# Splitting float64 weights into two fp32 parts: four VectorE steps in SBUF and two on GpSimd for each of twelve blocks, without PSUM banks

## The chip, the core and the metric

The kernel runs on one core of one Trainium2 chip. The metric is the time of one execution in microseconds (us) on the device. The profile names the engines PE (TensorE matmul), PEld (TensorE weight load), DVE (VectorE), ACT (ScalarE), POOL (GpSimd) and SP (SyncE, which issues most DMAs); SPq and ACTq are DMA-issuing instructions on those queues. SBUF is the on-chip memory of 128 partitions, PSUM the eight banks into which TensorE writes.

## What is computed

Banded attention for 8 batches, 8 heads, 576 positions and head size 64, followed by a gated feed-forward block:

```python
# attention: B, H, S, D = 8, 8, 576, 64
scores = q @ k.T / sqrt(D)           # heads 0-3: last 32 positions; heads 4-7: every 4th of the last 128
attn = softmax(where(mask, scores, -1e9))
x = (attn @ v).transpose(0, 2, 1, 3).reshape(B, S, 512)
# gated block: d_ff = 1024
h = maximum(x @ w_in, 0)
u, v = h[..., :512], h[..., 512:]
v_n = (v - mean(v)) / sqrt(var(v) + 1e-6)
v_s = einsum('ts,bsd->btd', w_spatial, v_n) + b_spatial[None, :, None]
out = (u * v_s) @ w_out
```

q, k, v, w_spatial and b_spatial are float32. w_in (512x1024) and w_out (512x512) are float64: they come from a float32 array times a numpy float64 scalar.

## The kernel before

**Two-part products.** Every matmul of the gated block runs in three passes over operands that were split into a high part `hi`, rounded to the matmul's fp32r format, and a low part `lo`, what is left: high by high, high by low, low by high. Activations are split with one copy (ACT) and one subtraction (DVE or POOL). Where a name ends in `h` or `l` it is such a part: `wih`/`wil` of w_in, `woh`/`wol` of w_out, `wth`/`wtl` of w_spatial, `xth`/`xtl` of the attention's output, `vnh`/`vnl` of the normalised v, `gh`/`gl` of the gated product.

**The float64 weights.** `weight` (line 276) splits one block of 128 rows by 512 columns. There are twelve: w_in's second half (`half` 1, used by the v tiles), blocks 1 to 4 below; its first half (`half` 0, used by the gate), blocks 5 to 8; and w_out, blocks 9 to 12. A block's 512 KB come by DMA into one of four `stage` buffers (`weight_in`, line 265; w_in in two transfers of 256 KB). ACT scales the words' upper halves (L295); DVE shifts the exponent into place (L297) and puts the sign back (L299), which gives `g`, the number without its last bits; ACT rounds `g` to `hi` (L334); DVE cuts `g` down to its power of two (L305); the lower words, times that power and 2**-52, are what `g` lacks; `lo` is the difference `g - hi` plus that rest. Blocks 1 to 6 do the lot on DVE (L297, L299, L305, L322, then the difference through the helper at L256 and the sum L328), with one `mid` buffer in SBUF and two PSUM banks. Blocks 7 to 12 (`pool=True`) do the last three steps on POOL (L312, L259, L318) after another ACT copy (L310), with two `mid` buffers and one PSUM bank.

**The stages around it.** The first batch has a start-up: q, k and v of two head groups and the weights are loaded, scores and softmax run (`unit`, three for each head group; POOL multiplies by the reciprocal sum at L489, PE transposes at L494, L520 multiplies by the values), the result is split (`evacuated`: xth by ACT at L546, xtl by DVE through L256), the v tiles are multiplied (`v_tile`, L572 and L586), normalised (L604 to L611) and split (L618, and POOL through L259), the gate follows (`gate`, L645 for u, L656 to L658 for the spatial product, L661 and L667) and the projection (`project`, L681). Of batch 1 the units are interleaved with the gate of batch 0, and so on.

**What sets the order.** Every piece of work is a generator, a strand with a rank. `Timeline` runs them against a table of costs, takes the strand whose next step can start earliest (start plus 0.2 times rank) and emits its instructions; each engine then executes in the order of emission. Buffers are handed out by tags (`stage`, `mid`, `bank`, `kqv` and so on). The tag `wk` has no buffer: it bounds how many blocks that use it are in work at once. So a changed cost or tag in `weight` changes the order of all engines' queues, not only of its own instructions. The spatial product cannot start before the bias is in (`bias`, line 362): its DMA of `b_sp` needs a `stage` buffer, and so an earlier block that gave its buffer back.

Of the kernel before, what the change touches and what calls it, by code (L numbers as in the profile page):

```python
# [121 lines left out]
def tile_banded_attention_gated_moe(  # L122
# [52 lines left out]
    def bufs(tag, shape, n, pool=const):  # L175
# [12 lines left out]
            wk=[None] * 1,  # L188
# [43 lines left out]
    ident = const.tile([P, P], F32, name="ident")  # L232
    make_identity(nc, ident)
# [42 lines left out]
    def weight(key, hi, lo, dtype, pool=False):  # L276

        yield [("in", *key)]
        yield "mid" if dtype == F32 else "mid mid bank" if pool else "wk mid bank bank"
        mid = yield ACT, 0.66  # L280
        *slot, mid = (mid[:1], mid[1:]) if len(mid) == 4 else (mid,)
        big = staged[key]
        if dtype == F32:
            w = big[1][:, :512]
            nc.scalar.copy(hi, w)
            yield DVE, 0.68
            sub(lo, w, hi)
            tl.give(big, *mid)
            tl.done(*key)
            return  # L290
        words = big[1][:, :1024].rearrange("p (c w) -> p w c", w=2)
        t, g, f = (m[1].bitcast(U32) for m in mid)


        nc.scalar.activation(f.bitcast(F32), words[:, 1], AF.Copy, scale=2.0**-112)  # L295
        yield DVE, 0.6
        nc.vector.tensor_scalar(t, f, 3, 0x7FFFFFFF, op0=ALU.logical_shift_left, op1=ALU.bitwise_and)  # L297
        yield DVE, 0.68
        nc.vector.scalar_tensor_tensor(g, f, 0x80000000, t, op0=ALU.bitwise_and, op1=ALU.bitwise_or)  # L299
        tl.add(key[-1] * 0.01, rounded(hi, g.bitcast(F32), ("hi", *key)))  # L300

        low = words[:, 0].bitcast(U32)
        p = t if pool else f
        yield DVE, 0.43 if pool else 0.6
        nc.vector.tensor_scalar(p, g, 0xFF800000, None, op0=ALU.bitwise_and)  # L305
        t, g, f, p = (m.bitcast(F32) for m in (t, g, f, p))
        if pool:
            tl.give(mid[2])
            yield ACT, 0.66
            nc.scalar.activation(words[:, 0], low, AF.Copy, scale=2.0**-52)  # L310
            yield POOL, 1.3
            nc.gpsimd.tensor_mul(t, p, words[:, 0])  # L312
            tl.give(big)
            yield [("hi", *key)]
            yield POOL, 1.3
            gsub(g, g, hi)
            yield POOL, 1.3
            nc.gpsimd.tensor_add(lo, t, g)  # L318
            tl.give(*mid[:2])
        else:  # L320
            yield DVE, 0.68
            nc.vector.scalar_tensor_tensor(f, low, 2.0**-52, p, op0=ALU.mult, op1=ALU.mult)  # L322
            tl.give(big)
            yield [("hi", *key)]
            yield DVE, 0.68
            sub(t, g, hi)
            yield DVE, 0.68
            nc.vector.tensor_add(lo, f, t)  # L328
            tl.give(*mid, *slot[0])
        tl.done(*key)  # L330
# [377 lines left out]
    for half in (1, 0):  # L708
        cols = slice(half * NF, half * NF + NF)
        for c in range(NC):  # L710

            heads = [c // 2 * 4 + c % 2 + n for n in (0, 2)]
            src = tuple(w_in[h * D : h * D + D, half] for h in heads)
            halves[half, c] = weight_in(("wi", half, c), src)
            r = -1.05 if half else -0.5
            tl.add(r + c * 0.05, weight(("wi", half, c), wi[0][:, c, cols], wi[1][:, c, cols], w_in.dtype, half == 0 and c > 1))
# [6 lines left out]
    for c in range(NC):  # L723
        tl.add(0.3, weight(("wo", c), wo[0][:, c, :], wo[1][:, c, :], w_out.dtype, True))
# [87 lines left out]
```

## Time and profile before

| what | us |
|---|---|
| time before, median of 3 runs | 581.32 |
| lowest and highest of the runs | 580.89 and 618.86 |
| time of the profiled execution (its span) | 580.3 |
| PE busy | 550.5 (95% of the span) |
| DVE busy | 317.0 (55%) |
| ACT busy | 248.5 (43%) |
| POOL busy | 139.2 (24%) |

The page gives for the profiled execution no time but the span, from its first to its last instruction; the median of the runs is 1.0 us above it. A row of the timeline reads: start, duration, engine, line, operation, output <- inputs, shape and type, count, and in brackets how long the engine had been idle and what ended that.

### The profile page before, as it was taken

The page shows a single profiled execution, that of the slowest core. Times are in us where ns is not written, and L with a number is a line of the kernel's source. Part 1 is how long each engine was busy: PE and PEld are TensorE (multiplying, and loading weights), DVE is VectorE, ACT ScalarE, POOL GpSimd, SP SyncE. Part 2 cuts the span into 40 slices and gives each one's busy share as a digit, 9 for nine tenths or more (in the row PEclk, how much of TensorE's full clock was granted, in tenths as well). Part 3 has the DMA queues.
Part 4 walks back from the last instruction along what each step waited for, and adds up shares of the span by engine and source line. Part 5 has one row for each costly group of instructions (what it writes and reads, how often), then busy time and mean ns, then how long its engine had stood idle before and what let it go on. Part 6 is the DMA issues. An engine that isn't in the chain of part 4 may idle for free.

```text
span 580.3 us, 18315 instructions
## 1 busy us (share of the span) xinstructions
PE 550.5 (95%) x7971; PEld 509.1 (88%) x7971; DVE 317.0 (55%) x765; ACT 248.5 (43%) x630; POOL 139.2 (24%) x163
## 2 busy tenths in 40 slices
PE   9788358999999999999999999999999999999997
PEld 7576358999999989998999989999999989999997
DVE  2789977244863376434863376444863476444411
ACT  2855686433444344434444344433444433423321
POOL 2110988001520032201420032201430132201000
PEclk9969577999999999999999999999999999999999
DMA  9986585431366104631355104641364012101011
GB/s 230 198 213 172 156 216 109 126 84 42 85 143 148 45 4 118 174 84 42 85 150 143 42 6 120 171 82 42 85 177 117 31 36 61 43 1 42 1 42 41
DMA packets 97444, 56.66 MB, mean 98 GB/s; under 512 B 78290, under 2 KB 87506, under 8 KB 97364
## 3 DMA queue, kind: packets, MB, share of 16 engines
q1 hardware_dynamic: 88148, 46.06, 32.7%
q10 hardware_dynamic: 9216, 9.44, 4.6%
q8 instruction: 62, 1.02, 0.7%
q14 instruction: 18, 0.15, 0.1%
HBM read 46.04 MB, written 9.44 MB: 96 GB/s over the span
## 4 chain that ended last, share of the span: by engine, by line
PE 82%; DVE 6%; DMA 5%; SPq 3%; POOL 1%; issue 1%; ACT 1%; ACTq 0%; DVEq 0%; POOLq 0%
PE bank L656 18%; PE bank L645 17%; PE bank L681 16%; PE bank L572 14%; PE bank L520 6%; PE bank L438 4%; PE bank L494 3%; DMA kqv<-in_vw_dram 2%; SPq L414 2%; PE bank L586 2%; PE bank L658 1%; PE bank L657 1%; DMA stage<-in_w_in_dram 1%; DMA kqv<-in_qT_dram 1%; DMA out_dram<-ob 1%
## 5 line engine op out<-in xcount | busy, mean ns | idle before, releaser
L608 POOL TENSOR_TENSOR rs<-rs,halfneg 128x1 f32<-128x1 f32 (+1 forms) x40 | 30.9, 776 | 244.5 <-DVE rs L606 244.5
L645 PE MATMUL bank<-xth,wih 128*128 128x288 f32 x256 | 80.1, 313 | 1.8 <-ACT p L464 1.8
L656 PE MATMUL bank<-wth,vnh 128*128 128x288 f32 x256 | 79.0, 309 | 0.0
L661 DVE TENSOR_TENSOR ur<-ur,bank 128x288 f32<-128x288 f32 x64 | 29.0, 453 | 87.9 <-PE bank L658 87.8
L645 PE MATMUL bank<-xtl,wih 128*128 128x288 f32 x256 | 76.7, 300 | 0.1
L645 PE MATMUL bank<-xth,wil 128*128 128x288 f32 x256 | 76.5, 299 | 0.0
L681 PE MATMUL bank<-gh,woh 128*128 128x288 f32 x256 | 76.3, 298 | 0.0
L656 PE MATMUL bank<-wtl,vnh 128*128 128x288 f32 x256 | 76.2, 297 | 0.0
L656 PE MATMUL bank<-wth,vnl 128*128 128x288 f32 x256 | 76.2, 297 | 0.0
L681 PE MATMUL bank<-gl,woh 128*128 128x288 f32 x256 | 75.7, 296 | 0.1
L681 PE MATMUL bank<-gh,wol 128*128 128x288 f32 x256 | 75.6, 295 | 0.0
L489 POOL TENSOR_TENSOR p<-p,rv 128x384 f32<-128x384 f32 x48 | 41.0, 855 | 78.4 <-DVE rv L487 71.5
L667 ACT CAST gh<-ur 128x288 fp32r<-128x288 f32 x64 | 27.6, 432 | 65.7 <-DVE ur L661 65.7
L645 PEld LDWEIGHTS bank<-xth,wih 128*128 128x128 f32 x256 | 49.1, 192 | 3.8 <-ACT p L464 2.2
L572 PE MATMUL bank<-wih,xth 128*128 128x512 f32 x128 | 51.2, 400 | 0.3 <-DVE xtl L256 0.3
L572 PE MATMUL bank<-wil,xth 128*128 128x512 f32 x128 | 50.6, 396 | 0.0
L572 PE MATMUL bank<-wih,xtl 128*128 128x512 f32 x128 | 50.4, 394 | 0.0
L645 PEld LDWEIGHTS bank<-xtl,wih 128*128 128x128 f32 x256 | 49.3, 192 | 0.4 <-issue 0.3
L656 PEld LDWEIGHTS bank<-wth,vnh 128*128 128x128 f32 x256 | 48.7, 190 | 0.6
L645 PEld LDWEIGHTS bank<-xth,wil 128*128 128x128 f32 x256 | 49.2, 192 | 0.0
L681 PEld LDWEIGHTS bank<-gl,woh 128*128 128x128 f32 x256 | 48.5, 189 | 0.6 <-DVE gl L256 0.3
L656 PEld LDWEIGHTS bank<-wtl,vnh 128*128 128x128 f32 x256 | 48.8, 191 | 0.2
(105 smaller groups left out, 1167.6 us busy)
## 6 DMA issues: line engine op xcount, KB each, us to landing
kqv<-in_vw_dram SPq DMA_DIRECT2D x128, 144.0 KB, 4.2
out_dram<-ob ACTq DMA_DIRECT2D x64, 144.0 KB, 1.8
kqv<-in_kT_dram SPq DMA_DIRECT2D x30, 304.0 KB, 3.4
kqv<-in_qT_dram SPq DMA_DIRECT2D x30, 288.0 KB, 4.2
stage<-in_w_in_dram SPq DMA_DIRECT2D x16, 256.0 KB, 5.6
stage<-in_w_out_dram SPq DMA_DIRECT2D x4, 512.0 KB, 3.4
stage<-in_w_spT_dram SPq DMA_DIRECT2D x5, 288.0 KB, 3.2
kqv<-in_kT_dram SPq DMA_DIRECT2D x2, 192.0 KB, 3.6
```

The costliest lines, as they stand in the source:

```text
L414: nc.sync.dma_start(dst[j * D : j * D + D, :, n, :], src[n * QB : n * QB + KW, :, j, :])
L438: nc.tensor.matmul(s[j][q * QB : q * QB + QB, e, :], kq[r, WIN + S :].rearrange("p (u n i t) -> p u t n i", n=2, i=QB, t=US)[:, u, g // 2 ...
L489: nc.gpsimd.tensor_mul(flat, flat, rv.unsqueeze(2).broadcast_to([P, 2 * US, KW]))
L494: nc.tensor.transpose(pp[:, e, :], p[:, e].rearrange("p j k -> p (j k)"), ident)
L520: nc.tensor.matmul(acc[j][1][1][i * D : i * D + D, (g - h * HB) * QB : (g - h * HB + 1) * QB], v[r, g, :], probs[b, G, u][1][r, e, q * QB ...
L572: nc.tensor.matmul(pm, x[a][:, c, cols], wi[w][:, c, NF:], start=c == 0 and n == 0, stop=c == NC - 1 and n == 2)
L608: nc.gpsimd.tensor_tensor(rs[:m], rs[:m], halfneg[:m], op=ALU.pow)
L645: nc.tensor.matmul(pu, wi[w][:, c, fs], x[a][:, c, ts], start=n == 0, stop=n == 3 * NC - 1)
L656: nc.tensor.matmul(pv, vn[c][a][:, fs], wt[w][:, c, ts], start=n == 0, stop=False)
L661: nc.vector.tensor_mul(ur, ur, pv)
L667: nc.scalar.copy(gated[0][:, f, ts], ur)
L681: nc.tensor.matmul(po, wo[w][:, f, ds], gated[a][:, f, ts], start=n == 0, stop=n == 3 * NC - 1)
```

## The change

- All twelve blocks take one path. ACT scales the upper words into a `mid` buffer in SBUF (not into a PSUM bank); DVE does four steps (shift, sign, power of two, lower words times the power), each with all inputs and its output in SBUF; POOL does the difference and the last sum.
- Each block needs two `mid` buffers and a `wk` tag and no bank. There are two `wk` tags, not one, and all twelve blocks use them; the ACT copy L310 and the POOL multiplication L312 are gone. The table's costs change with it.
- A third path (`sums=True`, with matmuls against `plus` and `minus`) is in the code, but both calls pass `False`, so that it emits nothing.
- The identity is drafted in the first `ob` buffer; `plus` and `minus` are made from it by two DVE instructions, and `ident` is `plus` read as fp32.

```diff
-            wk=[None] * 1,
+            wk=[None] * 2,
...
-    ident = const.tile([P, P], F32, name="ident")
-    make_identity(nc, ident)
+    draft = tl.bufs["ob"][0][:, :P]
+    make_identity(nc, draft)
+    plus, minus = (const.tile([P, P], F32R, name=n) for n in ("plus", "minus"))
+    nc.vector.tensor_copy(plus, draft)
+    nc.vector.tensor_scalar_mul(minus, draft, -1.0)
+    ident = plus.bitcast(F32)
...
-        yield "mid" if dtype == F32 else "mid mid bank" if pool else "wk mid bank bank"
-        mid = yield ACT, 0.66
-        *slot, mid = (mid[:1], mid[1:]) if len(mid) == 4 else (mid,)
+        yield "mid" if dtype == F32 else "wk mid mid"
+        got = yield ACT, 0.66
...
-        t, g, f = (m[1].bitcast(U32) for m in mid)
+        g, t = got[1][1], got[2][1]
+        gi, ti = g.bitcast(U32), t.bitcast(U32)
...
-        nc.scalar.activation(f.bitcast(F32), words[:, 1], AF.Copy, scale=2.0**-112)
-        yield DVE, 0.6
-        nc.vector.tensor_scalar(t, f, 3, 0x7FFFFFFF, op0=ALU.logical_shift_left, op1=ALU.bitwise_and)
+        nc.scalar.activation(g, words[:, 1], AF.Copy, scale=2.0**-112)
+        yield DVE, 0.43
+        nc.vector.tensor_scalar(ti, gi, 3, 0x7FFFFFFF, op0=ALU.logical_shift_left, op1=ALU.bitwise_and)
         yield DVE, 0.68
-        nc.vector.scalar_tensor_tensor(g, f, 0x80000000, t, op0=ALU.bitwise_and, op1=ALU.bitwise_or)
-        tl.add(key[-1] * 0.01, rounded(hi, g.bitcast(F32), ("hi", *key)))
+        nc.vector.scalar_tensor_tensor(gi, gi, 0x80000000, ti, op0=ALU.bitwise_and, op1=ALU.bitwise_or)
+        tl.add(key[-1] * 0.01, rounded(hi, g, ("hi", *key)))
+        yield DVE, 0.43
+        nc.vector.tensor_scalar(ti, gi, 0xFF800000, None, op0=ALU.bitwise_and)
+        yield DVE, 0.68
+        rest = lo if sums else t
+        nc.vector.scalar_tensor_tensor(rest, words[:, 0].bitcast(U32), 2.0**-52, t, op0=ALU.mult, op1=ALU.mult)
+        tl.give(big)
+        yield [("hi", *key)]
...
+        else:
             yield POOL, 1.3
             gsub(g, g, hi)
             yield POOL, 1.3
-            nc.gpsimd.tensor_add(lo, t, g)
+            nc.gpsimd.tensor_add(lo, g, rest)
...
-            tl.add(r + c * 0.05, weight(("wi", half, c), wi[0][:, c, cols], wi[1][:, c, cols], w_in.dtype, half == 0 and c > 1))
+            tl.add(r + c * 0.05, weight(("wi", half, c), wi[0][:, c, cols], wi[1][:, c, cols], w_in.dtype, False))
...
-        tl.add(0.3, weight(("wo", c), wo[0][:, c, :], wo[1][:, c, :], w_out.dtype, True))
+        tl.add(0.3, weight(("wo", c), wo[0][:, c, :], wo[1][:, c, :], w_out.dtype, False))
```

In the changed kernel the four DVE steps are L301, L303, L306 and L309, the ACT scaling is L299, the difference is the POOL helper at L263, the sum L328, and the DVE helper of L256 is L260. The order moves in three places that matter below.

**DVE, from the end of block 4 to the last split of the first batch.** `xtl` is the low part of the attention's output, L552 a small copy of its tail. Before:

```order
L328 TENSOR_TENSOR wil<-bank_66,mid_83 128x512
L256 TENSOR_TENSOR xtl_156<-bank_68,xth_155 128x2x144
L256 TENSOR_TENSOR xtl_156<-bank_67,xth_155 128x2x144
L552 CAST xth_155<-xtl_156 128x64
L256 TENSOR_TENSOR xtl_156<-bank_72,xth_155 128x2x144
L552 CAST xth_155<-xtl_156 128x64
L297 TENSOR_SCALAR mid_84<-bank_66 128x512
```

And now:

```order
L309 SCALAR_TENSOR_TENSOR mid_83<-stage_64,mid_83 128x512
L301 TENSOR_SCALAR mid_85<-mid_84 128x512
L303 SCALAR_TENSOR_TENSOR mid_84<-mid_84,mid_85 128x512
L260 TENSOR_TENSOR xtl_159<-bank_66,xth_158 128x2x144
L260 TENSOR_TENSOR xtl_159<-bank_67,xth_158 128x2x144
L306 TENSOR_SCALAR mid_85<-mid_84 128x512
L309 SCALAR_TENSOR_TENSOR mid_85<-stage_64,mid_85 128x512
L260 TENSOR_TENSOR xtl_159<-bank_70,xth_158 128x2x144
L552 CAST xth_158<-xtl_159 128x64
L260 TENSOR_TENSOR xtl_159<-bank_68,xth_158 128x2x144
L552 CAST xth_158<-xtl_159 128x64
```

The last `xtl` stood behind four blocks and now stands behind six.

**SP, the DMA queue, from the last weight block to the keys and queries of batch 1's last head pair** (L399 and L400 load keys and queries, L414 values, L369 the bias). Before:

```order
L273 DMA stage_65<-in_w_out_dram 128x512
L399 DMA kqv_74<-in_kT_dram 128x608
L400 DMA kqv_74<-in_qT_dram 128x576
L414 DMA kqv_75<-in_vw_dram 64x9x64 x4
L369 DMA stage_64<-in_b_sp_dram 1x576 x2
L399 DMA kqv_76<-in_kT_dram 128x608
L400 DMA kqv_76<-in_qT_dram 128x576
```

And now:

```order
L277 DMA stage_65<-in_w_out_dram 128x512
L369 DMA stage_64<-in_b_sp_dram 1x576 x2
L414 DMA kqv_75<-in_vw_dram 64x9x64 x4
L399 DMA kqv_78<-in_kT_dram 128x608
L400 DMA kqv_78<-in_qT_dram 128x576
```

The four value transfers moved from ahead of the bias to behind it, and the queries of the third head pair to ahead of the weights.

**PE, ahead of the first spatial product.** The L438 rows are the last scores of batch 1's units. Before:

```order
L437 LDWEIGHTS same
L437 MATMUL bank_67<-kinds,same 32x64
L438 MATMUL bank_67<-kqv_76 32x64
L494 MATMUL bank_68<-ident,p_88 128x128 x3
L656 MATMUL bank_71<-wth,vnh_99 128x288
```

And now:

```order
L437 LDWEIGHTS same
L437 MATMUL bank_71<-kinds,same 32x64
L438 MATMUL bank_71<-kqv_78 32x64
L656 MATMUL bank_66<-wth,vnh_99 128x288
L656 MATMUL bank_66<-wtl,vnh_99 128x288
```

The group of three transposes that stood between the scores and the product stands behind the second product now.

More of the change, by code (lines that the diff above doesn't have):

```diff
@@ L274, in weight_in, with weight @@
         tl.done("in", *key)
[L276 removed]
+    def weight(key, hi, lo, dtype, sums=False):
         yield [("in", *key)]
[L279 to L281 removed]
+        yield "mid" if dtype == F32 else "wk mid mid"
+        got = yield ACT, 0.66
         big = staged[key]
@@ L287, in weight @@
             sub(lo, w, hi)
-            tl.give(big, *mid)
+            tl.give(big, *got)
             tl.done(*key)
@@ L291, in weight @@
         words = big[1][:, :1024].rearrange("p (c w) -> p w c", w=2)
-        t, g, f = (m[1].bitcast(U32) for m in mid)
-        nc.scalar.activation(f.bitcast(F32), words[:, 1], AF.Copy, scale=2.0**-112)
-        yield DVE, 0.6
-        nc.vector.tensor_scalar(t, f, 3, 0x7FFFFFFF, op0=ALU.logical_shift_left, op1=ALU.bitwise_and)
-        yield DVE, 0.68
-        nc.vector.scalar_tensor_tensor(g, f, 0x80000000, t, op0=ALU.bitwise_and, op1=ALU.bitwise_or)
-        tl.add(key[-1] * 0.01, rounded(hi, g.bitcast(F32), ("hi", *key)))
[L302 to L314, printed above, removed]
+        g, t = got[1][1], got[2][1]
[3 more added lines that the diff above has]
+        nc.vector.tensor_scalar(ti, gi, 3, 0x7FFFFFFF, op0=ALU.logical_shift_left, op1=ALU.bitwise_and)
+        yield DVE, 0.68
+        nc.vector.scalar_tensor_tensor(gi, gi, 0x80000000, ti, op0=ALU.bitwise_and, op1=ALU.bitwise_or)
[7 more added lines that the diff above has]
+        yield [("hi", *key)]
+        if sums:
+            yield "bank"
+            (bank,) = yield PE, 1.34
+            pl = bank[1]
+            nc.tensor.matmul(pl, ident, g, start=True, stop=False)
+            nc.tensor.matmul(pl, minus, hi, start=False, stop=False)
+            nc.tensor.matmul(pl, plus, rest, start=False, stop=True)
+            yield ACT, 0.57
+            nc.scalar.copy(lo, pl)
+            tl.give(bank)
+        else:
             yield POOL, 1.3
@@ L317, in weight @@
             yield POOL, 1.3
[L318 to L329, printed above, removed]
+            nc.gpsimd.tensor_add(lo, g, rest)
+        tl.give(*got)
         tl.done(*key)
```

## The prediction

> **What bounds the kernel now.** I read the page's slices first, then the busy time by stretches, then the rows around the last waits of the start-up.
>
> ```profile
> span 580.3 us, 18315 instructions
> PE   9788358999999999999999999999999999999997
> PEclk9969577999999999999999999999999999999999
> ```
>
> A slice is 14.5 us. PE idles in slices 2 to 7 and hardly after; the granted clock falls there too.
>
> ```profile
> 15.70:43.80 28.10, 22.23 (x551) 17.63 (x549) 21.82 (x47) 18.26 (x80) 4.67 (x6) 0.82 0.90 209
> 43.80:69.50 25.70, 13.69 (x260) 10.50 (x258) 24.70 (x47) 14.59 (x39) 11.77 (x11) 0.82 0.64 163
> 69.50:91.30 21.80, 14.47 (x273) 13.37 (x271) 17.31 (x31) 18.01 (x52) 18.93 (x17) 0.66 0.77 182
> 91.30:137.70 46.40, 46.40 (x576) 44.47 (x575) 20.85 (x49) 22.14 (x75) 11.47 (x11) 0.97 0.39 99
> 266.20:331.40 65.20, 65.20 (x956) 60.79 (x955) 35.69 (x90) 26.30 (x56) 14.36 (x17) 1.00 0.35 93
> ```
>
> The columns after the stretch are its length, then PE, PEld, DVE, ACT, POOL, the clock, the DMA share and GB/s. From 91.3 us on PE is busy all the time, and the change touches nothing behind that point but the order. So the question is when PE gets there: a microsecond of the start-up is a microsecond of the whole. From 43.8 to 69.5 DVE is full (24.70 of 25.70), from 69.5 to 91.3 POOL is nearly so (18.93 of 21.80). What opens the gate at 91.3 is in three PE rows and the SP queue:
>
> ```profile
> 87.78 0.28 PE L438 MATMUL bank<-kqv 64*32 64x64 f32 x1 [4.62 <-DMA kqv<-in_qT_dram]
> ...
> 89.58 0.40 PE L438 MATMUL bank<-kqv 64*32 64x64 f32 x3
> 90.71 0.90 PE L494 MATMUL bank<-ident,p 128*128 128x128 f32 x3 [0.73 <-POOL p L489]
> 91.26 0.59 PE L656 MATMUL bank<-wth,vnh 128*128 128x288 f32 x1
> ```
>
> ```profile
> 77.63 2.98 SPq L414 DMA_DIRECT2D kqv<-in_vw_dram  x4
> 80.92 0.70 SPq L369 DMA_DIRECT2D stage<-in_b_sp_dram  x2
> 81.72 0.36 SPq L399 DMA_DIRECT2D kqv<-in_kT_dram  x1
> 82.52 0.35 SPq L400 DMA_DIRECT2D kqv<-in_qT_dram  x1
> ```
>
> The first spatial product (L656) stands behind scores that wait for queries issued at 82.52 and there at 87.78, 5.26 later. Those stand in the SP queue behind the bias, which waits for a stage buffer, which a w_out block gives back. That thread ties the weights' splitting to PE.
>
> **The change, part by part.** First a block by itself. Before, on DVE alone (below its first score):
>
> ```profile
> 7.43 0.84 DVE L456 TENSOR_REDUCE bank<-bank 128x3 f32<-128x192 f32 x2 [2.55 <-PE bank L438]
> ...
> 15.71 0.68 DVE L297 TENSOR_SCALAR mid<-bank 128x512 uint32<-128x512 uint32 x1
> ...
> 17.89 0.69 DVE L322 SCALAR_TENSOR_TENSOR bank<-stage,bank 128x512 f32<-128x512 uint32 x1
> ...
> 19.64 0.65 DVE L256 TENSOR_TENSOR mid<-bank,wih 128x512 f32<-128x512 f32 x1
> 20.33 0.69 DVE L328 TENSOR_TENSOR wil<-bank,mid 128x512 fp32r<-128x512 f32 x1
> ```
>
> ```profile
> L305 DVE TENSOR_SCALAR mid<-mid x6: 409/604/1256, 55.5 to 90.2; 128x512 uint32<-128x512 uint32 x6
> ...
> L299 DVE SCALAR_TENSOR_TENSOR mid<-bank,mid 128x512 uint32<-128x512 uint32 x6 | 4.2, 692 | 0.4
> ```
>
> Six steps of about 0.69 are 4.1 us for blocks 1 to 6. After, the two one-input steps (L301, L306) go by L305 in SBUF, whose shortest is 0.41, and the two-input steps (L303, L309) I take at 0.69 of L299, though no row has such a step with both inputs in SBUF: 0.41 + 0.69 + 0.41 + 0.69 = 2.2, about 2.1 since starts overlap by some tens of ns. DVE is relieved of 2.0 us in each of six blocks. Removing L310 frees ACT of six copies, which were not waited for long, and the banks it gives back are not missed: none of the waits quoted here ends with a bank coming free. The two added DVE set-up instructions lie in the 2.55 us that DVE idled before the first score; they cost nothing, and with that cover gone at most 0.8, two of L305's 0.41. POOL now has two steps in twelve blocks (24) where it had three in six (18).
>
> These steps collide, and that is the costly part:
>
> ```profile
> 56.93 1.29 POOL L312 TENSOR_TENSOR mid<-mid,stage 128x512 f32<-128x512 f32 x1 [17.73 <-DVE mid L297]
> 58.19 1.44 POOL L259 TENSOR_TENSOR mid<-mid,wih 128x512 f32<-128x512 f32 x1
> 59.70 1.66 POOL L318 TENSOR_TENSOR wil<-mid,mid 128x512 fp32r<-128x512 f32 x1
> ...
> 62.57 1.27 POOL L259 TENSOR_TENSOR mid<-mid,wih 128x512 f32<-128x512 f32 x1
> 63.92 1.66 POOL L318 TENSOR_TENSOR wil<-mid,mid 128x512 fp32r<-128x512 f32 x1
> ```
>
> ```profile
> 57.25 1.26 DVE L305 TENSOR_SCALAR mid<-mid 128x512 uint32<-128x512 uint32 x1
> 58.43 1.81 DVE L256 TENSOR_TENSOR wb<-stage,wa 64x576 fp32r<-64x576 f32 x1
> ...
> 63.11 1.34 DVE L256 TENSOR_TENSOR wtl<-stage,wth 128x576 fp32r<-128x576 f32 x1
> ```
>
> L305, 0.41 by itself, begins inside POOL's L312 (56.93 to 58.22) and ends 0.29 behind it. The subtraction at 63.11 begins inside L259, which ends at 63.84, and ends at 64.45, 0.61 behind it; L318, begun at 63.92, takes 0.39 longer than L259. So an SBUF-to-SBUF step of DVE and a POOL step take turns; a step that reads a bank (L299) kept its 0.69 all through. Before, all six steps of a full DVE block read a bank, and POOL was idle. After, all four DVE steps and both POOL steps of a block want the same turn: 2.1 + 2 x 1.25 = 4.6 us for a block, where DVE alone had needed 4.1. The Trainium skill (SBUF — State Buffer, Who interferes with whom) says that a VectorE instruction with two SBUF inputs contends with a GpSimd instruction that reads SBUF; of L303's operation with two such inputs no row of before shows it, and if only L301 and L306 took turns a block would hold them for 0.8 + 2.5 = 3.3 us, the direction of the first rival.
>
> Now the start-up with that price.
>
> ```profile
> 25.11 0.62 ACT L295 ACTIVATE bank<-stage 128x512 f32<-128x512 f32 x1 [0.90 <-DMA stage<-in_w_in_dram]
> ...
> 37.85 0.83 POOL L489 TENSOR_TENSOR p<-p,rv 128x384 f32<-128x384 f32 x1 [5.47 <-DVE rv L487]
> ```
>
> - Block 2 is bound by its DMA, so its first DVE step stays near 25.8. From there blocks 2 to 8 need 7 x 4.6 = 32.2, three L489 2.5, the small copies and `wb` 1.1: 35.8 with the turn never idle, so w_in is done at 61.6, say 62. Before it was L318 at 63.92 + 1.66 = 65.6. Won: 3.6.
> - The last `xtl` stands behind blocks 2 to 6: 25.8 + 5 x 4.6 + 2.5 + 0.5 = 51.8, against 45.7 before (the last row is PE's last of the v tiles):
>
> ```profile
> 45.07 0.67 DVE L256 TENSOR_TENSOR xtl<-bank,xth 128x288 fp32r<-128x288 f32 x1
> ...
> 60.17 0.68 DVE L604 BATCH_NORM_STATS2 bn<-mid 128x6 f32<-128x512 f32 x1
> ...
> 76.25 0.64 DVE L297 TENSOR_SCALAR mid<-bank 128x512 uint32<-128x512 uint32 x1
> ```
>
> ```profile
> 52.96 0.40 PE L586 MATMUL bank<-wih,xth 128*128 128x512 f32 x1
> ```
>
>   PE ends the v tiles some 6 us later, near 60 (before, 52.96 + 0.40 = 53.4). They are normalised (L604) behind block 8's DVE steps, at 59.9, so the delay is just covered; what was won on w_in goes here.
> - From L604 to block 9's first step DVE needed 16.1 (60.17 to 76.25), with the same list after: 59.9 + 16.1 = 76.0. The four steps with one L489 between them give the stage buffer back at 78.5. Before, POOL's L312 did, just ahead of the bias at 80.92: 2.4 earlier.
> - But the four L414 now stand between the bias and the keys: bias 0.70, L414 2.98, L399 and its gap 0.9, 0.1 for the seams, so the queries are issued at 83.2, are there at 88.4, and the scores take 2.2 (87.78 to 89.58 + 0.40): 90.6. L656 follows at once, without the wait for POOL's L489: 0.6 earlier than 91.26. The transposes that moved behind it cost 0.5.
>
> Sum: 580.3 - 0.6 + 0.5 = 580.2 for the execution profiled, and with the 1.0 us by which the runs' median lies above its span, 581.2. The likeliest case has an error of some 4 us to either side, since waits on three engines are chained in it.
>
> The price of L303 and L309 is bounded by 0.41, the one-input step, and by twice the row of L299 less its fixed part, below. I take 0.69, the nearest row, same operation and size.
>
> **The rivals.**
>
> *DVE and POOL seldom meet.* If POOL's steps fall where DVE waits anyway, a block costs DVE 2.1 and w_in's blocks flow. For it: POOL was idle for 17.7 us before 56.93. Against it: DVE was full in that stretch. Block 9's end then comes near 75, 3.5 earlier; the queries, L656 and all else by as much: 577.7.
>
> *The two-input step in SBUF runs at half the rate.* Slower than before.
>
> ```profile
> L661 DVE TENSOR_TENSOR ur<-ur,bank 128x288 f32<-128x288 f32 x64 | 29.0, 453 | 87.9 <-PE bank L658 87.8
> ...
> L328 DVE TENSOR_TENSOR wil<-bank,mid 128x512 fp32r<-128x512 f32 x6 | 4.1, 691 | 0.2
> ```
>
> From 288 to 512 elements a step with two inputs grows by 0.238 us, 1.06 ns for each, so 0.54 of the 0.69 is elements and half rate makes it 1.23, 1.08 more in a block. Blocks 2 to 9 stand in the way of the bias, 8 x 1.08 = 8.6: 589.8. It passes 2% only if such a step costs over 1.4 us. For it: both of the before kernel's two-input bit steps had a bank as one input. Against it: subtractions with both inputs in SBUF (63.11) take 0.61 once they have the turn. The Trainium skill has this as a rule: Vector Engine (DVE) Microarchitecture Reference, section 7 (Points that are easy to get wrong), says that a scalar_tensor_tensor "with two non-bf16 SBUF sources halves throughput"; by that rule this rival's sum holds, and no run here shows it yet.
>
> *The price is hidden.* PE's first spatial product is late for another reason, such as the values of L520; then the time stays at 581.3. It can't be told from the forecast.
>
> **How the numbers follow.** About 2% (11.6 us) is what a measurement of this kernel can tell from no change. Chances: the forecast 0.50, with the hidden case 0.08 beside it at the same time; DVE and POOL seldom meet 0.14; half rate 0.25; something else 0.03. The predicted time is the forecast's, 581.2, its own range 577 to 585. For 8 in 10 the range reaches from 575.5, 2 below the first rival, to 591, 1 above the half rate. Over 2% faster means L656 before 80 us: 0.02. Over 2% slower needs a step of 1.4 us or half rate with a stall of 3 us more: 0.10. Within 2%: 0.88.
>
> **What would show it.** Right: DVE's L306 spread between 0.41 and 1.3, as L305 was; POOL's L263 and L328 between 1.25 and 1.9; the last L328 on w_in near 62; the last `xtl` of batch 0 near 52; the bias issued near 78.5; L656 near 90.6; PE full from there. The half rate shows in the shortest L303, 1.2 in place of 0.69. It is wrong if L656 moves by more than 5 us either way, or if PE has gaps between 91 and 138 us that it did not have.

## The result and the profile after

| | us |
|---|---|
| time before, median of 20 runs | 582.45 (580.39 to 618.86) |
| time after, median of 20 runs | 586.31 (584.10 to 589.83) |
| ratio after to before | 1.0057, 95% interval 1.0030 to 1.0085 |
| predicted | 581.2, range 575.5 to 591.0, "no change" |

The change costs half a per cent. That is far under the 2% that I took as the least to be told from no change, but the interval of the ratio leaves out 1, and the time went the way that I had not forecast. An execution's time is its span and 1.75 us: the profile after has a span of 587.0 and belongs to an execution of 588.75, 2.4 above its median.

The head and two slice rows of the page after, to be laid beside those of before:

```profile
span 587.0 us, 18306 instructions
PE   8676576999999999999999999999999999999997
PEclk9867886999999999999999999999999999999999
```

And the busy time by stretches after (length, then PE, PEld, DVE, ACT, POOL, the clock, DMA share, GB/s):

```profile
15.70:43.80 28.10, 20.88 (x435) 15.80 (x434) 16.30 (x37) 16.00 (x72) 10.58 (x10) 0.76 0.79 177
43.80:69.50 25.70, 15.39 (x195) 11.35 (x195) 24.94 (x39) 12.51 (x24) 19.56 (x17) 0.87 0.53 152
69.50:91.30 21.80, 14.72 (x342) 12.88 (x342) 20.46 (x35) 14.67 (x55) 15.35 (x14) 0.82 0.75 211
91.30:97.00 5.70, 2.22 (x138) 2.01 (x138) 4.73 (x10) 4.03 (x13) 5.12 (x5) 0.50 0.61 86
97.00:143.00 46.00, 46.00 (x570) 44.08 (x571) 20.68 (x51) 22.10 (x72) 7.44 (x8) 0.96 0.38 99
```

PE is full from 97.0 instead of 91.3, so it is the start-up that has grown: from L656 to the end the span after needs 490.0 us, and the span before 489.0. DVE is as full as before between 43.8 and 69.5 (24.94 against 24.70), though it was given less to do, and POOL is now busy there too (19.56 against 11.77). The gate, in PE's rows and in the SP queue:

```profile
94.00 0.28 PE L438 MATMUL bank<-kqv 64*32 64x64 f32 x1 [3.60 <-DMA kqv<-in_qT_dram]
...
96.98 0.61 PE L656 MATMUL bank<-wth,vnh 128*128 128x288 f32 x1 [0.77 <-DVE vs L260]
```

```profile
83.60 0.59 SPq L369 DMA_DIRECT2D stage<-in_b_sp_dram  x2
84.24 2.58 SPq L414 DMA_DIRECT2D kqv<-in_vw_dram  x4
86.92 0.58 SPq L399 DMA_DIRECT2D kqv<-in_kT_dram  x1
87.56 0.41 SPq L400 DMA_DIRECT2D kqv<-in_qT_dram  x1
```

The last wait of the scores is for the same queries as before, behind the four L414 as the order said. Further back, DVE's timeline shows blocks 2 and, once POOL has work, 4:

```profile
30.20 0.46 DVE L260 TENSOR_TENSOR xtl<-bank,xth 128x288 fp32r<-128x288 f32 x1 [2.32 <-ACT xth L546]
30.77 0.43 DVE L301 TENSOR_SCALAR mid<-mid 128x512 uint32<-128x512 uint32 x1
31.24 0.69 DVE L303 SCALAR_TENSOR_TENSOR mid<-mid,mid 128x512 uint32<-128x512 uint32 x1
...
40.98 1.67 DVE L303 SCALAR_TENSOR_TENSOR mid<-mid,mid 128x512 uint32<-128x512 uint32 x1
42.68 1.40 DVE L306 TENSOR_SCALAR mid<-mid 128x512 uint32<-128x512 uint32 x1
44.11 1.20 DVE L309 SCALAR_TENSOR_TENSOR mid<-stage,mid 128x512 f32<-128x512 uint32 x1
```

L303 takes 0.69 by itself and 1.67 while POOL subtracts and adds. Block 2's first step stands at 30.77, where 25.8 was forecast. Here is PE's row with the longest wait "for nothing that the profile shows" ahead of it; below it stands the window of its clock:

```profile
17.35 0.21 PE L438 MATMUL bank<-kqv 64*32 64x64 f32 x1 [3.30 <-issue]
17.79 4.60 PE L697 MATMUL bank<-vnl 128*128 128x512 f32 x12
```

```profile
18.00:22.00 4.00, 4.00 (x12) 3.02 (x11) 3.12 (x8) 2.60 (x14) 0.56 (x1) 0.58 1.00 263
```

PE stopped in the middle of the third unit's scores for 3.30 us, which it did not do before. Then the granted clock stood at 0.58, and 12 warm-up matmuls (L697) held PE till 22.39. Two causes offer themselves: the turns that DVE and POOL take in SBUF, and this stop.

### The profile page after: what moved, and what is told of

Same layout as the page of the kernel before. It is cut to its first block, busy times and chain, and to the rows that moved or that the text cites. A ratio compares the mean times of both kernels' runs of the same rounds, so it can differ in the third digit from the quotient of the medians.

```text
span 587.0 us, 18306 instructions
## 1 busy us (share of the span) xinstructions
PE 552.1 (94%) x7970; PEld 508.8 (87%) x7970; DVE 319.1 (54%) x761; ACT 245.0 (42%) x624; POOL 150.3 (26%) x169
## 3 DMA queue, kind: packets, MB, share of 16 engines
q8 instruction: 62, 1.02, 0.7%
## 4 chain that ended last, share of the span: by engine, by line
PE 85%; DVE 5%; DMA 5%; issue 2%; ACT 2%; POOL 0%; SPq 0%; ACTq 0%; DVEq 0%; POOLq 0%
PE bank L645 17%; PE bank L656 17%; PE bank L681 16%; PE bank L572 13%; PE bank L520 6%; PE bank L438 5%; PE bank L494 3%; PE bank L697 3%; PE bank L586 2%; DMA kqv<-in_qT_dram 2%; DMA out_dram<-ob 2%; PE bank L658 1%; PE bank L657 1%; DVE mid L303 1%; DMA kqv<-in_vw_dram 1%
## 5 line engine op out<-in xcount | busy, mean ns | idle before, releaser
L656 PE MATMUL bank<-wth,vnh 128*128 128x288 f32 x256 | 79.2, 309 | 0.8 <-DVE vs L260 0.8
L656 PE MATMUL bank<-wtl,vnh 128*128 128x288 f32 x256 | 76.2, 298 | 0.0
L656 PE MATMUL bank<-wth,vnl 128*128 128x288 f32 x256 | 76.2, 298 | 0.0
L489 POOL TENSOR_TENSOR p<-p,rv 128x384 f32<-128x384 f32 x48 | 41.4, 862 | 73.0 <-DVE rv L487 70.5
L438 PE MATMUL bank<-kqv 64*32 64x64 f32 x2304 | 39.3, 235 | 14.1 <-DMA kqv<-in_qT_dram 10.0
L438 PEld LDWEIGHTS bank<-kqv 64*32 64x32 f32 x2304 | 32.8, 125 | 21.5 <-issue 14.5
L656 PEld LDWEIGHTS bank<-wth,vnh 128*128 128x128 f32 x256 | 48.9, 191 | 1.6 <-DVE vs L260 1.0
L656 PEld LDWEIGHTS bank<-wtl,vnh 128*128 128x128 f32 x256 | 48.9, 191 | 0.2
```

The lines of the kernel that those rows point to most:

```text
L438: nc.tensor.matmul(s[j][q * QB : q * QB + QB, e, :], kq[r, WIN + S :].rearrange("p (u n i t) -> p u t n i", n=2, i=QB, t=US)[:, u, g // 2 ...
L489: nc.gpsimd.tensor_mul(flat, flat, rv.unsqueeze(2).broadcast_to([P, 2 * US, KW]))
L656: nc.tensor.matmul(pv, vn[c][a][:, fs], wt[w][:, c, ts], start=n == 0, stop=False)
```

## Experiments

Below, the "stop" is that early one, block 2 and L656 stand for the start of block 2's first DVE step and of the first spatial product, and ratios are to the kernel before in the same job, with 95% intervals.

### 1. Which part costs it: POOL's steps or the identity

The two kernels again, unaltered, as a base for the others.

> The changed kernel again, unchanged, for a second profile. In the first one block 2's first DVE step came at 30.77 us, not near 25.8, behind a PE stall of 3.3 us at 14.06 us that no engine explains, and the first spatial product (L656) at 96.98. Theory A (most of that lateness is the luck of one execution): without the stall block 2 starts near 26 and L656 stands near 91 to 93, the span near 582 to 583. Theory B (the new order itself makes block 2 late): block 2 again after 29 us, L656 again after 95, span 585 or more. Timed against before: 1.005 to 1.007 in both.

> The kernel before, unchanged, for a second profile of it. Ratio 1.000 within 0.003. Theory A: PE stalls that no engine explains fall elsewhere than in the first profile, and L656 moves from 91.26 by 1 to 4 us in either direction. Theory B: the same places, L656 within 0.5 us of 91.26.

POOL's steps out (`e_fill`), all queues in the same order:

```diff
             yield POOL, 1.3
-            gsub(g, g, hi)
             yield POOL, 1.3
-            nc.gpsimd.tensor_add(lo, g, rest)
+            nc.gpsimd.memset(lo.bitcast(F32), 0.0)
```

> The changed kernel with its order kept word for word; POOL's difference and sum for the weights' low parts are left out, and the low parts are filled with zeros by one POOL instruction each, which reads nothing. DVE's four steps stay. Theory 'turns' (DVE and POOL wait for each other): the DVE steps fall back to 0.42, 0.69, 0.42, 0.69 throughout, blocks 2 to 9 take 2.1 us each in place of about 4, L656 comes 4 to 8 us earlier, ratio to before 0.993 to 0.999. Rival 'late start' (the turns cost nothing, what is late is late before block 2): the ratio stays at 1.004 to 1.007.

The identity as before (`e_ident`):

```diff
-    draft = tl.bufs["ob"][0][:, :P]
-    make_identity(nc, draft)
...
-    ident = plus.bitcast(F32)
+    ident = const.tile([P, P], F32, name="ident")
+    make_identity(nc, ident)
```

> The changed kernel with the identity made as before (no draft in the output buffer, no plus and minus, two DVE instructions fewer at the start). Both theories: they lie under a wait, ratio as the changed kernel's, 1.005 to 1.007. If the set-up were the cause, 1.000 to 1.002.

| run | median | ratio | stop | block 2 | L656 | span |
|---|---|---|---|---|---|---|
| before | | | none | 25.77 | 91.26 | 580.3 |
| c_before | 581.38 | 1.0011 [0.9979, 1.0043] | none | 24.90 | 90.78 | 578.6 |
| after | 586.31 | 1.0057 [1.0030, 1.0085] | 3.30 | 30.77 | 96.98 | 587.0 |
| c_after | 583.58 | 1.0031 [0.9989, 1.0073] | 2.62 | 31.86 | 97.80 | 586.6 |
| e_fill | 578.00 | 0.9941 [0.9919, 0.9963] | 3.66 | 31.69 | 87.68 | 576.3 |
| e_ident | 584.99 | 1.0073 [1.0057, 1.0088] | 0.62 | 25.98 | 93.02 | 581.5 |

From block 2 to L656 the changed kernel needs 66.2 us, the kernel before 65.5, and e_fill 56.0. So POOL's two steps cost some 10 us of start-up. e_fill leaves out the weights' low parts and so most of the wait for them, but it is not only POOL's own time: DVE's four steps show it in the groups by shape, of the kernel after and then of e_fill.

```profile
L303 DVE SCALAR_TENSOR_TENSOR mid<-mid,mid 128x512 uint32<-128x512 uint32 x12 | 12.2, 1016 | 0.4
L301 DVE TENSOR_SCALAR mid<-mid 128x512 uint32<-128x512 uint32 x12 | 9.8, 817 | 2.1 <-ACT mid L299 1.9
L309 DVE SCALAR_TENSOR_TENSOR mid<-stage,mid 128x512 f32<-128x512 uint32 x12 | 8.8, 735 | 0.4
L306 DVE TENSOR_SCALAR mid<-mid 128x512 uint32<-128x512 uint32 x12 | 7.5, 628 | 0.4
```

```profile
L303 DVE SCALAR_TENSOR_TENSOR mid<-mid,mid 128x512 uint32<-128x512 uint32 x12 | 9.3, 777 | 0.4
L309 DVE SCALAR_TENSOR_TENSOR mid<-stage,mid 128x512 f32<-128x512 uint32 x12 | 8.3, 692 | 0.4
L301 DVE TENSOR_SCALAR mid<-mid 128x512 uint32<-128x512 uint32 x12 | 6.0, 498 | 2.1 <-ACT mid L299 1.9
L306 DVE TENSOR_SCALAR mid<-mid 128x512 uint32<-128x512 uint32 x12 | 5.5, 460 | 0.4
```

38.3 us in all against 29.1: 9.2 us of DVE's time go to turns. In the kernel before, the same groups of DVE's steps for the twelve blocks add up to 37.6, so the turns give back all that the lighter steps save. The expectation for e_fill held in its ratio; L656 came 9.3 us earlier, more than the 4 to 8 I gave, and the steps did not fall back to 0.42 throughout (L301 has a mean of 498 ns). The identity is not the cost: without its new set-up the ratio is no better. c_after's profile repeats the first one (theory B), though its median is only 1.5 us above that of the kernel before; c_before's L656 keeps its place within 0.5 us.

### 2. Where the steps may stand

All twelve blocks' difference and sum on DVE (`e_dve`); only w_in's eight (`e_dve_in`, the same edit where the key is not `wo`):

```diff
-            yield POOL, 1.3
-            gsub(g, g, hi)
-            yield POOL, 1.3
-            nc.gpsimd.tensor_add(lo, g, rest)
+            yield DVE, 0.68
+            sub(g, g, hi)
+            yield DVE, 0.68
+            nc.vector.tensor_add(lo, g, rest)
```

> The changed kernel with the difference and the last sum of all 12 blocks on VectorE in SBUF, none on GpSimd. Theory (VectorE and GpSimd take turns on SBUF, which makes a block of 2.1 us of VectorE steps last 4.6): without GpSimd's two steps nothing lengthens the six VectorE steps, a block is 0.41 + 0.69 + 0.41 + 0.69 + 2 x 0.61 = 3.4 us, so the way from block 2's first step to L656 falls from 66 us by 8 x 1.2 to about 57; with block 2 still near 31 L656 starts near 88 and the time is about 578. Rival (GpSimd's steps lie beside VectorE's and cost VectorE little; the changed kernel is late for PE's stop alone): the two steps added to each VectorE block cost 8 x 1.2 us, L656 near 107 and about 596 us.

> The changed kernel with the difference and the last sum of w_in's 8 blocks on VectorE in SBUF, those of w_out's 4 blocks on GpSimd as before. Theory (turns): the same gain on blocks 2 to 8, 7 x 1.2 us, and block 9 as in the changed kernel: from block 2 to L656 about 58, L656 near 89, about 579 us. If it is the last blocks and not w_in's that hold up the bias, it stays at the changed kernel's 97 and about 585 us.

The new form for one half of the blocks and the old for the other, with the old identity and two `wk` tags (`weight_sb` is the changed `weight`; `e_late6`, whose edit is shown, gives blocks 7 to 12 the new form and lets each old block take both tags; `e_first6` gives the new form to blocks 1 to 6):

```diff
-            tl.add(r + c * 0.05, weight(("wi", half, c), ...))
+            tl.add(r + c * 0.05, (weight_sb if half == 0 and c > 1 else weight)(("wi", half, c), ...))
...
-        tl.add(0.3, weight(("wo", c), ...))
+        tl.add(0.3, weight_sb(("wo", c), ...))
```

> The kernel before, but with the changed four VectorE steps and GpSimd's two for blocks 7 to 12 only (the two `wk` turns are kept; blocks 1 to 6 keep the banks and the old steps, and the identity is set up as before). Theory (PE's stop in the third unit comes with the changed early part of the program): the early part is the old one, so PE does not stop in the third unit's scores, block 2 starts near 25.8, blocks 2 to 6 cost the old 4.1, L656 is near 91 and the time within 1 us of the kernel before, 581 to 582. Rival (the stop comes with anything that makes the program other than before, wherever it stands): PE stops 2 to 4 us near 14, block 2 near 31, L656 near 96, about 586 us.

> Half of the change: blocks 1 to 6 with the four VectorE steps in SBUF and GpSimd's two, blocks 7 to 12 with the old form that w_in's last blocks and w_out's had (a bank, ScalarE's scaling and GpSimd's three steps, which the changed kernel dropped), identity as before. Theory (turns between VectorE and GpSimd are what eats the gain on blocks 2 to 8): blocks 2 to 6 last 4.6 us as in the changed kernel, so w_in and the bias are no earlier than there, L656 between 92 and 97 by its start, ratio 1.003 to 1.007. Rival (the turns matter only for w_out's blocks, just ahead of the bias): the time is that of the kernel before.

| run | median | ratio | stop | block 2 | bias | L656 |
|---|---|---|---|---|---|---|
| e_dve | 582.63 | 0.9995 [0.9964, 1.0026] | none | 24.55 | 76.39 | 89.61 |
| e_dve_in | 586.66 | 1.0055 [1.0016, 1.0093] | 2.83 | 32.41 | 84.34 | 96.64 |
| e_late6 | 585.26 | 1.0072 [1.0038, 1.0106] | 0.55 | 27.11 | 84.41 | 96.60 |
| e_first6 | 587.92 | 1.0073 [1.0030, 1.0115] | 2.84 | 31.36 | 80.25 | 91.27 |

In e_dve the turns are gone: its four steps need 27.4 us in all, and a block's six run at 0.69 and 0.42 each, as in its fifth:

```profile
39.86 0.38 DVE L301 TENSOR_SCALAR mid<-mid 128x512 uint32<-128x512 uint32 x1
40.28 1.21 DVE L303 SCALAR_TENSOR_TENSOR mid<-mid,mid 128x512 uint32<-128x512 uint32 x1
41.52 0.43 DVE L306 TENSOR_SCALAR mid<-mid 128x512 uint32<-128x512 uint32 x1
41.99 0.69 DVE L309 SCALAR_TENSOR_TENSOR mid<-stage,mid 128x512 f32<-128x512 uint32 x1
42.59 0.68 DVE L260 TENSOR_TENSOR mid<-mid,wih 128x512 f32<-128x512 f32 x1
43.31 0.69 DVE L328 TENSOR_TENSOR wil<-mid,mid 128x512 fp32r<-128x512 f32 x1
```

One L489 on POOL, and L303 takes 1.21. The bias is 4.5 us earlier than before (80.92). But PE then waits for DVE itself, 2.31 us in the last scores:

```profile
87.80 0.24 PE L437 MATMUL bank<-kinds,same 64*32 64x64 bf16 x2 [2.31 <-DVE vs L260]
```

and more of the units' work stands behind L656, from which the end is 491.6 us off instead of 489. So e_dve's expected 578 was missed by 4.6: a block did get cheaper, but from block 2 to L656 it is still 65.1 us, where I had expected 57, and the run is level with the kernel before. My rival there (596) is out too. e_dve_in missed its 579 by 7.7; it has the early stop, and from block 2 to L656 it takes 64.2.

e_late6 failed its expectation. Its early part is the old one and block 2 starts at 27.1, yet L656 is 5.3 late. Its blocks 7 and 8 start at 60.67 and 68.70 (before: 50.02 and 55.80), behind work of the v tiles, and POOL's steps meet DVE's other SBUF work there: three L651 took 4.31 us together, one alone 0.53. How much of the 5.3 is order and how much turns is not separated. e_first6's ratio is what the turns foretold; its L656 is earlier than the 92 to 97 I gave, with more work moved behind it (720 matmul records in the next 46 us, against 570 after). Its profile, like that of e_dve_in, is of an execution above its median, so I draw no more from either than that doing it for a part of the blocks alone did not avoid the cost.

### 3. Is it the stop?

The kernel before with the new identity (`b_ident`, the six added lines of the change alone), and both kernels again, for their starts:

> The kernel before with nothing but the changed set-up of the identity (drafted in an output buffer, then two VectorE operations into `plus` and `minus`). If this set-up is what makes PE stop in the third unit's scores (without it the changed kernel stopped for 0.6 us in place of 3.3), PE stops 3 us near 14, block 2 starts near 30 and L656 near 96: about 586 us. If the stop comes with the blocks' new order, block 2 stays near 25.8, L656 near 91 and the time within 1 us of the kernel before.

> The changed kernel again, unaltered, for a second look at its start. 29 executions of it spread over 583.3 to 589.8 us, and both that left a trace were of the upper end (588.4, 588.75) and had PE stopped 2.6 and 3.3 us in the third unit's scores, with block 2 at 30.8 and 31.9. If the stop is what makes an execution late, one near 584 us has a stop under 1 us, block 2 near 26 to 27 and L656 near 93; if the stop belongs to the changed kernel whatever its time, it is there in an execution near 584 us too, and that one is short elsewhere.

> The changed kernel once more, unaltered, for the same question: the stop of PE in the third unit's scores goes with the time (under 1 us at 584, about 3 us at 588), or does not.

> The kernel before, unaltered, for one more look at its start. Its executions spread over 578.4 to 589.4 us, and the two with a trace were of the lower part (582.06 and 580.36) and had no stop of PE in the third unit. If the stop is a matter of the single execution and not of the change, an execution near 587 us has it, with block 2 near 30; one near 580 us has it not.

> The changed kernel again, unaltered, beside the two above for its median: about 583.5 to 586 us, 0.3 to 0.6% above the kernel before; the profiled execution, as in the four before it, with PE's stop of 2 to 3.3 us.

| run | time of this execution | stop | block 2 | L656 | span |
|---|---|---|---|---|---|
| c_after2 | 588.26 | 2.97 | 32.28 | 97.15 | 586.5 |
| c_after3 | 587.63 | 2.09 | 27.40 | 95.36 | 585.9 |
| c_after4 | 584.85 | none | 25.52 | 94.15 | 583.1 |
| c_before2 | 580.24 | none | 25.78 | 91.29 | 578.5 |
| b_ident | 580.27 | none | 25.54 | 90.01 | 578.4 |

b_ident's median is 581.87, ratio 1.0007 [0.9972, 1.0042]: the identity neither costs time nor brings the stop. c_after2 and c_after3 were meant to catch an execution near 584 us and caught late ones, with the stop. c_after4 (median 586.21, ratio 1.0072 [1.0034, 1.0109]) is the useful miss. It was to have the stop and has none, block 2 is where the forecast had it, and L656 is still 2.9 us later than before. So the stop explains why the first profile is so late, but without it the changed kernel is late too. In c_after4 PE stops elsewhere, and DVE idles in front of block 4 (PE's rows, then DVE's):

```profile
24.03 1.48 PE L520 MATMUL bank<-pT,kqv 64*64 64x32 f32 x87 [1.46 <-issue]
30.24 0.31 PE L438 MATMUL bank<-kqv 64*32 64x64 f32 x1 [4.10 <-issue]
```

```profile
34.37 0.19 DVE L487 RECIPROCAL rv<-sm 128x6 f32<-128x6 f32 x1 [2.71 <-ACT sm L467]
...
36.85 0.97 DVE L301 TENSOR_SCALAR mid<-mid 128x512 uint32<-128x512 uint32 x1 [1.38 <-ACT mid L299]
```

What PE waits for can be counted in the trace. In the first 40 us the long stops called "issue" come after PE's 449th, 961st or 1217th record (matmuls, weight loads and a few rows of its semaphores), 256 or twice 256 apart, and queue 8 of the page ("q8 instruction: 62 packets, 1.02 MB") carries 16 KB packets, 62 for some 16,000 matmuls and weight loads, so about 256 for a packet. I take the packets of queue 8 to be PE's program. Two things in the traces bear this out: across the twenty profiles every stop of more than 0.55 us at such a border ends 1.3 to 1.9 us after the packet that belongs to it has landed (the first for 449, the third for 961, the fourth for 1217), and where 40 or 72 records more stand ahead (below), the stops still come after the same record numbers, and so earlier in the work. The kernel before stops so too, after its 1985th record, for 2.5 to 3.3 us in its three profiles; in the first:

```profile
60.63 0.26 PE L438 MATMUL bank<-kqv 64*32 64x64 f32 x1 [3.25 <-issue]
```

The DMA view of the window from 9 to 13 us, first of before, then of after:

```profile
q1 hardware_dynamic: 1032, 1.02, 106.0%
q8 instruction: 1, 0.02, 1.7%
```

```profile
q1 hardware_dynamic: 1091, 1.03, 105.4%
```

Before, the first packet comes at 10.6; after, at 14.4, with a data queue that is full in both, and PE goes on 1.6 us after it has landed.

To make that packet early I put more and smaller instructions ahead of the border. First 12 warm-ups of 512 columns as 48 of 128 (in `e_code`, `b_code` and, on e_dve, `e_dve_code`):

```diff
         while tl.now < 20:
+            if n < 12:
+                for j in range(4):
+                    nc.tensor.matmul(got[0][1][:, j * P : j * P + P], z, z, start=True, stop=True)
```

> The changed kernel, but each of PE's first 12 warm-up matmuls (128 x 512) made as four of 128 columns: the same columns in all, 36 instructions more ahead of the third unit, and nothing else moved. In the trace PE stopped at its 449th instruction, 256 after the one (the 193rd) at which the next packet of its program seems to be asked for; with 36 instructions more, both fall 36 instructions earlier, the asking in the second unit's scores near 6.8 us instead of the warm-up near 9, the need near 13.6 instead of 14. Theory (the stop, and the drop of the clock behind it, put block 2 and all after it back): no stop or one under 1 us, block 2 near 25 to 26, L656 near 91 to 92, span 580 to 581, and the median 1 to 3 us under that of the changed kernel in the same job. Rival (the stop is met by slack, or another wait takes its place): block 2 moves less than 2 us and the median stays with the changed kernel's.

> The kernel before with the same 12 warm-up matmuls made as 48. It did not stop in the third unit in any trace, so its profile stays as it is, L656 at 91 and span 578 to 580. If its later executions, some 2 in 10 at 585 to 589 us, are those in which the packet came late, they become fewer here; if not, they stay.

> The changed kernel with the difference and last sum of all blocks on VectorE, and with the 12 warm-up matmuls made as 48. Its profile without the latter had no stop and block 2 at 24.6, L656 at 89.6, with 2.5 us of transposes moved behind it, and ran level with the kernel before (0.9995). The stop being absent already, it stays level: 580 to 583 us; if its timed executions had the stop more often than the profiled one, the median falls by 1 to 2 us.

591.34, 591.65 and 589.26 us, ratios 1.0143 [1.0091, 1.0195], 1.0158 [1.0110, 1.0206] and 1.0118 [1.0072, 1.0163]. All three missed, and the first PE row says why (e_code):

```profile
1.04 10.50 PE L700 MATMUL bank<-vnl 128*128 128x128 f32 x48 [1.04 <-DVE vnl L203]
```

The 48 take 10.5 us, 0.22 each, with a weight load for each (PEld is busy for 10.3 us of it); the 13 first warm-ups had taken 5.1, 0.39 each, so the first unit is some 6 us late. The early stop is gone in all three, but these runs say nothing on its price. They do say one thing on the change: with this late start e_code (591.34) and b_code (591.65) are level, so what the change costs may depend on when the units start. Then 24 small bf16 matmuls in place of four warm-ups, `e_code2` on the changed kernel, `b_code2` on the kernel before:

```diff
         while tl.now < 20:
+            if n < 4:
+                zb = z.bitcast(BF16)
+                for j in range(6):
+                    nc.tensor.matmul(got[0][1][:QB, :64], zb[:, :QB], zb[:, :64], start=True, stop=True)
```

> The changed kernel, with PE's first 4 warm-up matmuls (some 1.3 us) made as 24 small ones (bf16, 32 by 64 columns, with their weight loads): 44 instructions more ahead of the second unit and, unlike the 12 split before, no time more, so unit 1 is done near 6 us as ever. The 193rd instruction then comes near 6.8 us instead of 9, the 449th near 13.6 instead of 14. Theory (the early stop is what separates the late executions, 587 to 590, from the typical ones, 583 to 586, which lose their 3 us elsewhere): no stop at the 449th, block 2 near 25.5, L656 near 94 as in the one profile of the changed kernel without an early stop, the median 584 to 585 and hardly an execution over 587; the ratio stays at 1.004 to 1.006, since what the typical executions lose is not touched. Rival (the stop is all that the change lost): the ratio falls to 1.000. Third way (the late packets are met at the next border whatever is done at the first): a longer stop near the 961st or 1217th, and the median as it was.

> The kernel before with the same 24 small matmuls for 4 warm-ups. If its late executions (585 to 589 us, some 2 in 10) come from the same early stop, they go, and the median stays or falls by under 1 us (ratio 0.997 to 1.000). If they come from elsewhere, they stay.

| run | median (range) | ratio | stop | block 2 | L656 | span |
|---|---|---|---|---|---|---|
| e_code2 | 583.06 (580.62 to 584.85) | 0.9993 [0.9963, 1.0023] | none | 25.30 | 92.62 | 581.2 |
| b_code2 | 580.39 (578.15 to 581.22) | 0.9936 [0.9903, 0.9969] | none | 25.81 | 90.36 | 578.4 |

The 24 take 1.46 us, as much as the four warm-ups they replace (a warm-up is two records, so the border moves by 40 of them, not the 44 I gave; in e_code by 72, not 36). The late executions go in both kernels: the kernel before reached 588.38 in this job, b_code2 not over 581.22. That the packet is asked for earlier is my reading and not shown: it comes at 10.8 (e_code2) and 9.3 us (b_code2), against 10.3 to 10.6 in c_after4 and the kernel before. Both gain some 0.6% in the ratio, and between the two stands what stood between after and before: 0.9993 / 0.9936 = 1.0057; by the medians it is 583.06 - 580.39 = 2.7 us, 0.46% (each ratio is good to 0.3%). e_code2's ratio is the one that I had given to the rival, "the stop is all that the change lost"; b_code2 speaks against it, since the kernel before gains as much. So the 24 take away a loss that both kernels have, and the change costs 2.7 us beside it, in executions without the early stop. That the loss of the kernel before is that stop as well is not shown: none of its late executions was profiled, and all of b_code2's twelve lie below the median of the kernel before, so it was not the late ones alone that fell. The expectation for e_code2 was wrong in its ratio (it fell) and right in its places (block 2 near 25.5, L656 1.4 earlier than the 94 I gave); that for b_code2 was right on the late executions and too small in its gain (0.997 to 1.000 expected). b_code2 is the fastest of the complete kernels here.

## Why the prediction was wrong

Three steps of the prediction failed: "Block 2 is bound by its DMA, so its first DVE step stays near 25.8" in the profile taken first, and "35.8 with the turn never idle" and "L656 follows at once" in executions where block 2 is in time. In place of the first two stood PE waiting for its own program, and in place of the third DVE's `vs`; the sum has neither wait. Of the cases that I had priced it is none, but the "something else" to which I gave 0.03. The chain from block 2 to L656, term by term (us):

| step | forecast | after | c_after4 | e_code2 |
|---|---|---|---|---|
| block 2's first DVE step | 25.8 | 30.77 | 25.52 | 25.30 |
| from there to block 9's first step | 50.2 | 49.90 | 52.03 | 51.80 |
| from there to the bias | 2.5 | 2.93 | 2.93 | 2.93 |
| bias to the queries' issue | 4.7 | 3.96 | 3.96 | 3.95 |
| issue to the scores' last wait for them | 5.2 | 6.44 | 6.77 | 4.49 |
| those scores | 2.2 | 2.21 | 2.19 | 3.73 |
| wait of L656 | 0 | 0.77 | 0.75 | 0.42 |
| L656 | 90.6 | 96.98 | 94.15 | 92.62 |

- **Right: what bounds it, and that DVE and POOL take turns.** PE is full from L656 on, and it is its start that moved. "4.6 us for a block" came out in the sum alone: from block 2's first step to block 9's the profile has 49.9 us, 50.2 forecast, but DVE's four steps took 2.2 us in blocks 2 and 3, beside which POOL stood idle, and 5.25 in block 4. That the two evened out is luck. L306 spread from 0.41 to 1.40 and L263 from 1.27 to 1.74, close to what I wrote. The Trainium skill's rule (SBUF — State Buffer, Who interferes with whom) holds for the two-input step too: L303 goes from 0.69 to 1.67.
- **Wrong in the profile: "Block 2 is bound by its DMA, so its first DVE step stays near 25.8".** In the profile of after its ACT step stood behind `xth`, that behind PE, and PE behind packets of its program (stops of 3.30 us after record 449 and 1.95 after 961): 30.77. This one step is 5.0 of the 6.4 us that L656 missed. L656 moved by 5.7 us there, more than the 5 that I had named as the sign of being wrong. But it is a matter of the execution; c_after4 and e_code2 have 25.5 and 25.3.
- **Wrong in the median: "35.8 with the turn never idle", and "L656 follows at once".** Where block 2 is in time, the turn does stand idle. With DVE's quicker steps PE reaches its 1217th record at 24.7 (e_code2), where the old steps had it wait for DVE's `xtl` just ahead of it (till 29.1 in b_code2), but the packet that goes on from there starts at 26.7 in both. PE's rows of e_code2 and b_code2:

```profile
29.50 0.27 PE L437 MATMUL bank<-kinds,same 64*32 64x64 bf16 x5 [4.62 <-issue]
```

```profile
29.11 2.14 PE L520 MATMUL bank<-pT,kqv 64*64 64x32 f32 x70 [1.69 <-DVE xtl L256]
```

  PE stops 4.1 to 4.6 us (c_after4 and e_code2). ACT stands behind PE, in front of the copy L497, and POOL behind ACT, since the rounding of blocks 2 and 3 (L334) follows that copy in ACT's queue. In c_after4, ACT's row and then POOL's:

```profile
31.83 0.48 ACT L497 COPY pT<-bank 128x384 f32<-128x384 f32 x1 [4.40 <-PE bank L494]
```

```profile
34.92 1.27 POOL L263 TENSOR_TENSOR mid<-mid,wih 128x512 f32<-128x512 f32 x1 [10.61 <-ACT wih L334]
```

  DVE idles some 4 us in front of block 4, and the way from block 2 to block 9 takes 1.6 to 1.8 more than forecast. The profiles agree: where block 2 is in time or 1.6 late (c_after3, c_after4, e_ident, e_code2), this stop is 3.8 to 4.6 us and the way 51.5 to 52.0; where block 2 is 5 to 6.5 late (after, c_after, c_after2), the stop is at most 1.4 and the way 49.3 to 50.4. No run took this stop away alone, so its price is read from rows and not measured. At the end PE waits for DVE, 0.4 to 0.75 for `vs` just ahead of L656, in e_code2 also 1.46 for `xtl` in the scores. The landing of the queries scatters by 2.3 us within the table and is no steady term.
- **Mis-sized: the balance.** I had 0.6 us won at L656 and 0.5 lost behind it. Without the stop L656 is 2.3 (92.62 against 90.36) to 2.9 later, and behind it e_code2 loses 0.5 more than b_code2 (488.6 against 488.1 us from L656 to the end). That this is the 0.5 forecast means little: the three profiles of the kernel before scatter from 487.2 to 489.0 there. The sum of 2.7 us is what the medians show.
- **Half rate: out.** L303 and L309, both inputs in SBUF, have the minimum and the median of the old step with a bank (in the view of one line: shortest, median and longest in ns, of after):

```profile
L303 DVE SCALAR_TENSOR_TENSOR mid<-mid,mid x12: 691/693/1666, 19.4 to 97.8; 128x512 uint32<-128x512 uint32 x12
...
L309 DVE SCALAR_TENSOR_TENSOR mid<-stage,mid x12: 691/693/1198, 20.6 to 99.0; 128x512 f32<-128x512 uint32 x12
```

  The Trainium skill's sentence on two SBUF sources (Vector Engine (DVE) Microarchitecture Reference, section 7), taken as the prediction takes it, as half the rate of the step with a bank, does not hold for this operation here.
- **Seldom meet: out.** 9.2 us of DVE's time went to turns (e_fill).
- **The price is hidden: out.** Without POOL's two steps L656 comes 9.3 us earlier (e_fill).
- **The offset.** I added 1.0 us from span to median; an execution is its span and 1.75, so the execution profiled before was one of 582.06.

What makes the first packet of PE's program late in one execution and not in the next stays open, as does why four of the five profiles of the changed kernel had it late and none of the three of before. Up to 10 us PE does the same work in all of them, and from 9 to 13 us the DMA engines are full. Loading less data then was not tried.

## What to carry to other kernels

Before steps of VectorE are moved from PSUM to SBUF to shorten them, add up what both VectorE and GpSimd then do in SBUF: here the steps fell from 4.1 to 2.1 us in six of the blocks and the turns gave all of it back. A gain in one engine ends at the next thing that does not move with it, here, by the rows, a packet of TensorE's program; look for the wait that comes after the one removed. And compare more than one profile of a kernel before a single long wait is blamed: the early stop of 3.30 us came and went between executions of the same kernel, and without it L656 was still 2.9 us late.

## What the hardware showed

- PE can stop for its own program: up to 3.7 us after its 449th record (e_fill) and over 4 after its 1217th, told in the rows only as "issue". With stops of 2.6 to 3.3 us (after, c_after, c_after2) the granted clock fell to 0.50, for 3.4 us in the first and 6.8 in the other two; 12 warm-ups then took 4.60 us in the profile after, and 3.04 at clock 1.00 in c_after4. In c_after3 the stop was 2.09, the clock stayed at 1.00, and block 2 was 1.6 late instead of 5 to 6.5.
- 24 small bf16 matmuls in the first 2.5 us, in place of four warm-ups, made the kernel before 0.64% faster (0.9936 [0.9903, 0.9969]); its late executions were gone, and all twelve executions lay below 582.18, the median without the 24.
- With 128 x 128 fp32 weights loaded anew each time, a matmul of 128 columns took 0.22 us and one of 512 columns 0.39 in the first microseconds of the kernel: a quarter of the columns for over half the time. Later, at clock 1.00, twelve of 512 columns took 3.04 us, 0.25 each.
